# FFT convolution on one core: four weight differences half a round later, one plane burst half a round sooner, the first inverse jobs from half round 13

## The chip, the cores and the metric

The kernel runs on one core of a Trainium2 chip. The metric is the device time of one execution in microseconds. The core has five engines that run their own instruction streams: TensorE (PE, matrix products into PSUM; its weight loads are PEld), VectorE (DVE), ScalarE (ACT), GpSimd (POOL) and SyncE (SP), which issues nearly all DMAs here. An instruction that depends on another engine waits on a semaphore, and everything behind it on its own engine waits with it.

## The reference

The input `x` is 1 x 224 x 224 x 96 in bfloat16, the weights `w` are 7 x 7 x 96 x 96. Both are transformed over the image axes, multiplied per frequency with a sum over the input channels, and transformed back: a circular 7 x 7 convolution.

```python
wp = jnp.pad(w, ((0, H - K), (0, W - K), (0, 0), (0, 0)))
Xf = rfft2(x, axes=(1, 2))
Wf = rfft2(wp, axes=(0, 1))
Yf = jnp.einsum('bhwi,hwio->bhwo', Xf, Wf)
y = irfft2(Yf, s=(H, W), axes=(1, 2)).astype(jnp.bfloat16)
```

## The kernel before

The kernel does not transform the whole image. It splits the height into 8 blocks of 28 rows and works along the height with a short real transform of length 32 and two rows treated apart, which makes 17 "slots" s (slot 0 holds the two real frequencies, slots 1 to 15 are complex, slot 16 holds the two rows), and along the width it computes a direct 7-tap convolution in a two-phase form with few products. The width is split into 7 tiles t of 32 columns. For each tile there are four kinds of work:

- forward jobs (`f_jobs` for the first three tiles, `a_jobs` for the others): TensorE multiplies a loaded piece of x (`xn`) by the transform `Fm` into a PSUM bank, and `evac` copies the bank to `xf` on VectorE or ScalarE, whichever has the smaller running cost (the table `load`, to which VectorE's and ScalarE's other work is added as well);
- plane jobs (`jit`): three VectorE instructions per group of slots (`JGB`: 0-2, 3-5, 6-8, 9-11, 12-14, 15-16) that make sums and differences of `xf` in one of three buffers `J`;
- rounds (`b_round`): the products of one slot (TensorE, 33 matmuls of 96 columns for a complex slot), and their combination: ScalarE scales a part (`tt_`), VectorE makes `u` and `v` from PSUM, GpSimd adds them into `yf` (the y sum). After a group of slots `yf` is stored to the scratch `scr` in memory;
- inverse jobs (`c_jobs`): a transposed piece of the scratch (`tt`) is loaded, multiplied by the inverse transform `Gm` (two matmuls of 384 columns a job), evicted to `yo` and stored to the output. `yo` lies partly in the third J buffer, so the profile shows some as J. When a job is the last of its load, `pump` issues the next load.

The weights are transformed on the chip too. `prep_jobs` fill the first two of the three parts of each slot's weights `WF` (TensorE and an eviction), and `diff(i)` (line 400) makes the third part of slot i, the difference of the other two, in one VectorE instruction of 96 x 960. It adds 560 to VectorE's running cost.

The first two tiles run interleaved: in round r the first tile does slot r and the second tile slot r-4 (`LAG`). I call the two halves (r,0) and (r,1); rounds 4 to 16 have both. The filling work is put into half rounds by a small planner: `add(a, b, jobs)` spreads jobs over half rounds a to b (`pace`, line 828), and `fills` emits what is due. In the rounds that have both halves, (r,0) has the number 2r and (r,1) has 2r+1, and all that is due is emitted at `mid` (line 659): after VectorE's `u` and ahead of the products b1 and of VectorE's `v`. From the third tile on, one tile runs alone and slot s has the half rounds 2s (at `mid`) and 2s+1 (at `end`).

Per complex half round TensorE does: b0, with four matmuls on J, eight on xf (the last four use the difference) and seven on J (these use the third plane job); the fills; and b1, fourteen on J. VectorE does u, the fills that fall to it, v, and the plane jobs of a burst. Program order is kept on every engine (`_Ordered`).

A burst is one group's plane jobs: `bursts` (lines 851-859) gives the half round in which the first two instructions are emitted, behind `v`; the third follows in the next half round (`rest`, line 911). In a half round with two plane jobs the y sum on GpSimd is made to wait for them (line 677). The bursts around the change are: first tile, slots 9-11 in (7,1), 12-14 in (10,1), 15-16 in (13,1); second tile, slots 12-14 in (15,0), 15-16 in (16,0).

Difference i (5 to 15) is emitted in half round 2i-2, that is at the middle of (i-1,0) (line 866), and first used in (i,0). The loads of the first tile's scratch are issued in round 20 (`queue_c(0)`, line 904). While the third tile runs alone (t = 2), the 11 inverse jobs of the first tile are spread over half rounds 10 to 34 (lines 936-940, `CQ[2]` is (11, 0)).

Of the kernel before, what the change touches and what calls it, by code (L numbers as in the profile page):

```python
# [17 lines left out]
NS = L // 2  # L18
# [22 lines left out]
JGB = ((0, 3), (3, 6), (6, 9), (9, 12), (12, 15), (15, 17))  # L41
# [18 lines left out]
def slot(s, part):  # L60
    return S5[s][part] if s < len(S5) else 3 * s - 1 + part
# [3 lines left out]
def kernel(  # L65
# [10 lines left out]
    TL = NT - 1  # L76
# [67 lines left out]
    def dma(out_ap, in_ap):  # L144
        return DE.dma_start(out=out_ap, in_=in_ap)
# [43 lines left out]
    def load_x(t, jg):  # L189
        return load_rows(xbuf(t, jg), jg, t * 2 * TW, 2 * TW)  # L190
# [209 lines left out]
    def diff(s):  # L400
        def f():
            load["v"] += 60 + C * NTAP / 1.92
            w0, w1, w2 = (WF[0:C, slot(s, r)].rearrange("i t o -> i (t o)") for r in range(3))
            VE.tensor_tensor(out=w2, in0=w0, in1=w1, op=ALU.subtract)
        return f
# [69 lines left out]
    def new_xf(t, s0=0, s1=NS):  # L475
        xf = xf_bufs[t % 2]
        xf_tiles[t] = xf
        if t > 0:
            prev = xf_tiles[t - 1]
            for ph in range(2):  # L480
                o, i = (v[0:C, ph, :, s0:s1, p:p + HALO, :].rearrange("c r s w j -> c r s (w j)") for v, p in ((xf, 0), (prev, TW)))
                apart(("A", t), ("halo", s0), SE.copy(out=o, in_=i))
                load["a"] += 160 + 0.85 * 2 * (s1 - s0) * HALO * NJ
        return xf
# [34 lines left out]
    def then_load(f, t, jg):  # L519
        def g():  # L520
            f()
            if t < NT:
                load_x(t, jg)
        return g
# [11 lines left out]
    def f_jobs(t, part):  # L536
        s0, s1 = (SH0, SH2, SH3)[t][part:part + 2]
        n = 2 * (s1 - s0) * JG
        nr = -(-TW * n // 512)
        e = [-(-TW * i // nr) for i in range(nr + 1)]  # L540
        fv = Fm[:, :, s0:s1].rearrange("p r s j -> p r (s j)")

        def mk_(jg, a, b, ph):
            def f():
                pa = bank()
                for k in range(b - a):
                    i = 2 * (a + k) + ph
                    TE.matmul(pa[:, k * n:(k + 1) * n], lhsT=xbuf(t, jg)[:, i * C:i * C + 128], rhs=fv, start=True, stop=True)
                xo = xf_tiles[t][0:C, ph, :, s0:s1, HALO + a:HALO + b, jg * JG:(jg + 1) * JG]
                pi = pa[0:C, 0:(b - a) * n].rearrange("c (w r s j) -> c r s w j", r=2, s=s1 - s0, w=b - a)  # L550
                return apart(("A", t), (a, jg, ph, part), evac(xo, pi, (b - a) * n))
            return f
        return [[mk_(jg, a, b, ph) for a, b in zip(e[:-1], e[1:]) for ph in range(2)] for jg in range(2)]
# [247 lines left out]
    def queue_c(t):  # L801
        pend.extend((t, *k) for k in (LT if t < TL - 1 else LTL))
        pump()
# [32 lines left out]
    def fills(qs, k):  # L836
        def f():
            for q in qs:
                pace(q, k)
        return f  # L840
# [3 lines left out]
    def add(a, b, jobs):  # L844
        qs.append([a, b, jobs, len(jobs)])
# [5 lines left out]
    bursts = {}  # L851
    rest = []
    for g in range(len(JGB)):
        g0 = JGB[g][0]
        if g:
            bursts[(g0 - 2, 1 if g0 - 2 >= LAG else 0)] = (0, g)
        r1 = LAG + g0 - (3 if g == len(JGB) - 1 else 1)
        bursts[(r1, 0 if r1 < NS else 1)] = (1, g)
    bursts[(NS + LAG - 3, 1)] = (2, 0)
    nburst = len(bursts)  # L860
    for r in range(NS + LAG):
        if r == 0:
            for i in range(1, PGRP[0][1]):
                add(max(2 * i - 3, 0), 2 * i - 1, [diff(i)])
            for i in range(N5, REAL[1]):
                add(2 * i - 2, 2 * i, [diff(i)])
            add(0, 4, fj[1][0] + fj[1][1])
            add(8, 12, fj[2][0] + fj[2][1])
        if r == 2:
            new_xf(1, SH2[0], SH2[1])  # L870
        for p in range(3):
            if r == (1, 3, 6)[p]:
                if p:
                    new_xf(1, SH2[p], SH2[p + 1])
                else:
                    xf_tiles[1] = xf_bufs[1]
                fj = f_jobs(1, p)
                if p == 2:
                    for jg in range(2):
                        fj[jg][-1] = then_load(fj[jg][-1], 2, jg)  # L880
                add((4, 7, 12)[p], (7, 11, 15)[p], fj[0] + fj[1])
        for p in range(2):
            if r == SH3[p + 1] + 1 - p:
                new_xf(2, SH3[p], SH3[p + 1])
                fj = f_jobs(2, p)
                if p:
                    for jg in range(2):
                        fj[jg][-1] = then_load(fj[jg][-1], 3, jg)
                add(2 * r, 2 * r + (12, 5)[p], fj[0] + fj[1])
        if r == PGRP[-2][1] + 1:  # L890
            assert not any(q[2] for q in qs[:len(PGRP) - 1])
            wtmp_cm.__exit__(None, None, None)
            t_pool = ctx.enter_context(tc.tile_pool(name="tt", bufs=NTT, side="right"))
            t2_pool = ctx.enter_context(tc.tile_pool(name="tt2", bufs=1, side="right"))
            yo_pool = ctx.enter_context(tc.tile_pool(name="yo", bufs=2, side="right"))
            g_pool = ctx.enter_context(tc.tile_pool(name="gp", bufs=1, side="right"))
            GA = g_pool.tile([KA, 4 * B], BF16, name="GA")
            GB = g_pool.tile([128, 2, 4 * B], BF16, name="GB")
            GE.memset(GA[:], 0.0)
            GE.memset(GB[:], 0.0)  # L900
        if r == 3:
            g_fin()
        if r == NS + 3:
            queue_c(0)
        for t in range(2):
            s = r - LAG * t
            if not 0 <= s < NS:
                continue
            now = bursts.pop((r, t), ())
            now = jit(*now) if now else []  # L910
            now, rest = rest + now[:2], now[2:]
            both = LAG <= r < NS
            b_round(t, s, fills(qs, 2 * r + (t if both else 0)), fills(qs, 2 * r + (t if both else 1)), False, now)
            if r == 0:
                for d in load_x(1, 1):
                    tc.add_manual_dep(d.ins, held_x.ins.name, SYNC, reason="second half behind the first products")
# [8 lines left out]
    for t in range(2, NT):  # L925
        if t == TL:
            scr_tiles[t] = None
            scr_tiles[(t, 0)] = dr_pool.tile([TW, NJ, SA, 4 * C], BF16, name="scra")
            for i in range(2):
                scr_tiles[(t, 1 + i)] = dr_pool.tile([TW, NJ, (SB - SA, NS - SB)[i], 4 * C], BF16, name=f"scrb{i}")  # L930
        else:
            scr_tiles[t] = dr_pool.tile([TW, NJ, NS, 4 * C], BF16, name="scr")
        qs = []
        if t + 1 < NT:
            add(4 if t == 2 else 0, 26, a_jobs(t + 1))
        nold, nnew = CQ[t]
        k1 = 2 * NS if t < TL else 2 * NS - 8
        k0 = {2: 10, TL: 6}.get(t, 3)
        km = k0 + -(-(k1 - k0) * nold // (nold + nnew))
        add(k0, km, cj[:nold])  # L940
        cn = c_jobs(t - 1)
        cj = cn[nnew:]
        add(km, k1, cn[:nnew])
        plan = {}
        for g, (s0, s1) in enumerate(JGB):
            if g + 1 < len(JGB) or t + 1 < NT:
                plan[s0 if g + 1 < len(JGB) else s0 - 1] = g
        for s in range(NS):
            now = ()
            if s in plan:  # L950
                g = plan[s]
                now = jit(t, g + 1) if g + 1 < len(JGB) else jit(t + 1, 0)
            if s == (3 if t in (2, TL) else 2):
                queue_c(t - 1)
            if t in (3, 4):
                next(gp, None)
            if t == TL and s == SA + 2:
                sv = scr_tiles[(TL, 0)].rearrange("w j s (r e) -> (j s r) w e", r=2)
                for g in range(2):
                    for p0, p1 in ((0, 64), (64, KA)):  # L960
                        dma(tl_a[g][p0:p1], sv[g * KA + p0:g * KA + p1])
            b_round(t, s, fills(qs, 2 * s), fills(qs, 2 * s + 1), bool(now) or (t == TL and s >= NS - 3), now)
# [70 lines left out]
```

## Time and profile before

| what | us |
|---|---|
| median of 3 runs | 266.95 |
| lowest and highest | 266.09, 269.16 |
| profiled execution | 266.45 |
| its span | 264.7 |
| TensorE busy | 249.9 |
| VectorE busy | 219.5 |
| ScalarE busy | 196.2 |
| GpSimd busy | 98.6 |
| granted TensorE clock | 0.999 of full speed |

Times within the execution are counted from the start of the span. In a timeline, a line gives the start, the time from the first start to the last end, the engine, the line, the operation with output and inputs, how many instructions are merged, and in brackets the idle time of the engine before it and what ended it. All instructions show L99, the helper that keeps the order, so they are told apart by their tiles: WF<-WF is a difference, J<-xf and J<-J are plane jobs, yf<-v,u is a y sum, pb<-tt,Gm is an inverse job. In the profile round (8,0) has its u at 50.77, (11,0) at 63.44, (14,0) at 75.63, and (5,0) at 37.07.

### The profile page before, as it was taken

To read this page: it belongs to the slowest core of one execution; us is meant where nothing else is said; L and a number is where in the kernel's file an instruction comes from. 1 tells how busy PE (TensorE), PEld (TensorE's weight loads), DVE (VectorE), ACT (ScalarE), POOL (GpSimd) and SP (SyncE) were. 2 spreads that over 40 slices of the span, in tenths; PEclk is the share of its full clock that TensorE was granted. 3 is DMA by queue.
4 is the path that set the end of the run, shared out by engine and by line. 5 is a ranking of instruction groups with operands and counts; after the bars stand their busy time and mean duration, and the time that the engine had idled before them with its cause. 6 is when DMAs were issued, how large, how long until landed. Compare 5 with 4: busy or idle time off the path is not lost.

```text
span 264.7 us, 11951 instructions
## 1 busy us (share of the span) xinstructions
PE 249.9 (94%) x5041; PEld 232.0 (88%) x5041; DVE 219.5 (83%) x465; ACT 196.2 (74%) x467; POOL 98.6 (37%) x152
## 2 busy tenths in 40 slices
PE   8988999999998997999999999999999999999793
PEld 3978999999998996999999998999999999989472
DVE  6989898899899685778887888878989799989734
ACT  8979887787834966998988789897988853453433
POOL 7784134464655523323223232334123423424000
PEclk9999999999999999999999999999999999999999
DMA  7994105511113594997976596989689342858896
GB/s 184 275 190 112 47 6 157 157 47 47 50 46 122 145 233 86 276 302 205 304 211 210 140 279 193 249 242 308 204 167 272 103 138 83 224 171 203 227 247 207
DMA packets 46929, 46.77 MB, mean 177 GB/s; under 512 B 35340, under 2 KB 38104, under 8 KB 46876
## 3 DMA queue, kind: packets, MB, share of 16 engines
q1 hardware_dynamic: 46156, 44.54, 61.3%
q10 hardware_dynamic: 720, 1.47, 1.6%
q8 instruction: 39, 0.64, 1.0%
q14 instruction: 14, 0.11, 0.1%
HBM read 24.66 MB, written 21.33 MB: 174 GB/s over the span
## 4 chain that ended last, share of the span: by engine, by line
PE 70%; DVE 8%; DMA 7%; ACT 5%; issue 5%; POOL 2%; SPq 1%; DVEq 0%; POOLq 0%; ACTq 0%
PE pb L99 68%; DMA tt<-scr 5%; DVE J L99 3%; DVE v L99 2%; ACT xf L99 2%; PE ps L99 2%; ACT WF L99 2%; POOL ct L99 2%; DMA out_dram<-yo 1%; DVE WF L99 1%; SPq L99 1%; POOL yf L99 1%; DVE u L99 1%; DVE yf L99 0%; DVE wq L99 0%
## 5 line engine op out<-in xcount | busy, mean ns | idle before, releaser
L99 PE MATMUL pb<-WF,J 96*128 96x96 bf16 x2821 | 162.6, 206 | 2.5 <-DVE J L99 2.3
L99 PEld LDWEIGHTS <-J 96*128 96x128 bf16 x2821 | 137.4, 98 | 11.4 <-DVE J L99 3.6
L99 POOL TENSOR_TENSOR yf<-v,u 128x384 bf16<-128x384 f32 x79 | 81.7, 1046 | 140.8 <-issue 80.0
L99 ACT CAST xf<-pb 96x408 bf16<-96x408 f32 (+6 forms) x140 | 65.1, 491 | 3.5 <-PE pb L99 1.5
L99 PE MATMUL pb<-WF,xf 96*128 96x96 bf16 x952 | 60.1, 206 | 0.9 <-ACT WF L99 0.9
L99 DVE TENSOR_TENSOR J<-xf 96x456 bf16<-96x456 bf16 (+3 forms) x85 | 56.6, 705 | 0.0
L99 PEld LDWEIGHTS <-xf 96*128 96x128 bf16 x952 | 47.3, 98 | 1.4 <-ACT xf L99 0.8
L99 PE MATMUL pb<-Fm,xn 118*128 118x136 bf16 (+4 forms) x576 | 43.7, 203 | 0.9 <-ACT WF L99 0.9
L99 PE MATMUL pb<-tt,Gm 102*84 102x384 bf16 (+1 forms) x132 | 31.9, 326 | 2.5 <-DMA tt<-scr 1.8
L99 ACT CAST yo<-pb 84x384 bf16<-84x384 f32 (+1 forms) x59 | 25.2, 480 | 8.9 <-PE pb L99 5.6
L99 ACT CAST J<-pb 84x384 bf16<-84x384 f32 (+1 forms) x63 | 27.3, 491 | 4.9 <-PE pb L99 2.6
L99 PEld LDWEIGHTS <-xn 118*128 118x128 bf16 x576 | 28.6, 97 | 1.1 <-issue 0.9
L99 DVE TENSOR_TENSOR J<-J 96x912 bf16<-96x912 bf16 (+2 forms) x42 | 24.4, 580 | 0.0
L99 ACT CAST WF<-pb 96x480 bf16<-96x480 f32 x42 | 21.1, 561 | 0.3 <-PE pb L99 0.2
L99 PEld LDWEIGHTS <-wq 128*128 128x128 bf16 (+1 forms) x288 | 19.7, 149 | 0.7 <-ACT wq L99 0.7
L99 DVE TENSOR_TENSOR yf<-v,u 128x384 bf16<-128x384 f32 x26 | 15.1, 582 | 0.9
L99 PE MATMUL pb<-wq 128*128 128x120 bf16 x192 | 15.3, 224 | 0.0
L99 PEld LDWEIGHTS <-Gm 102*84 102x84 bf16 (+1 forms) x132 | 11.5, 117 | 4.1 <-issue 2.1
L99 DVE TENSOR_TENSOR WF<-WF 96x960 bf16<-96x960 bf16 x15 | 13.8, 918 | 1.4 <-ACT WF L99 1.3
L99 ACT COPY xf<-xf 96x816 bf16<-96x816 bf16 (+4 forms) x18 | 10.8, 652 | 0.0
L99 PEld LDWEIGHTS <-wu 128*112 128x112 bf16 (+1 forms) x36 | 4.6, 130 | 4.8 <-issue 2.5
L99 POOL TENSOR_SCALAR J<-J 102x1 f32<-102x1 f32 (+1 forms) x24 | 7.6, 316 | 1.8
(397 smaller groups left out, 252.6 us busy)
## 6 DMA issues: line engine op xcount, KB each, us to landing
scr<-yf SPq DMA_DIRECT2D x30, 288.0 KB
xn<-in_x_dram SPq DMA_DIRECT2D x12, 672.0 KB
tt<-scr SPq DMA_DIRECT2D x24, 336.0 KB
out_dram<-yo SPq DMA_DIRECT2D x12, 252.0 KB
out_dram<-J SPq DMA_DIRECT2D x12, 252.0 KB
tt<-scr SPq DMA_DIRECT2D x6, 288.0 KB
WF<-in_x_dram SPq DMA_DIRECT2D x2, 672.0 KB
out_dram<-tt SPq DMA_DIRECT2D x8, 168.0 KB
```

The costliest lines, as they stand in the source:

```text
L99: r = fn(*a, **k)
```

## The change

Three lines change. Differences 6, 9, 12 and 15 are emitted in half round 2i-1, at the middle of (i-1,1), instead of 2i-2. The second tile's burst for slots 12-14 is emitted in (14,1) instead of (15,0) (its third instruction in (15,0) instead of (15,1)); the other entries of `bursts` keep their values, since every r1 is below NS. The first tile's 11 inverse jobs are spread over half rounds 13 to 34 of the third tile instead of 10 to 34.

```diff
@@ -855,7 +855,7 @@
         if g:
             bursts[(g0 - 2, 1 if g0 - 2 >= LAG else 0)] = (0, g)
         r1 = LAG + g0 - (3 if g == len(JGB) - 1 else 1)
-        bursts[(r1, 0 if r1 < NS else 1)] = (1, g)
+        bursts[(r1 - 1, 1) if g == len(JGB) - 2 else (r1, 0)] = (1, g)
     bursts[(NS + LAG - 3, 1)] = (2, 0)
     nburst = len(bursts)
     for r in range(NS + LAG):
@@ -863,7 +863,7 @@
             for i in range(1, PGRP[0][1]):
                 add(max(2 * i - 3, 0), 2 * i - 1, [diff(i)])
             for i in range(N5, REAL[1]):
-                add(2 * i - 2, 2 * i, [diff(i)])
+                add(2 * i - (1 if i % 3 == 0 else 2), 2 * i, [diff(i)])
             add(0, 4, fj[1][0] + fj[1][1])
             add(8, 12, fj[2][0] + fj[2][1])
         if r == 2:
@@ -935,7 +935,7 @@
             add(4 if t == 2 else 0, 26, a_jobs(t + 1))
         nold, nnew = CQ[t]
         k1 = 2 * NS if t < TL else 2 * NS - 8
-        k0 = {2: 10, TL: 6}.get(t, 3)
+        k0 = {2: 13, TL: 6}.get(t, 3)
         km = k0 + -(-(k1 - k0) * nold // (nold + nnew))
         add(k0, km, cj[:nold])
         cn = c_jobs(t - 1)
```

## The prediction

> **What bounds the kernel now.** I read the page first, then TensorE's timeline for its idle times, then VectorE's and GpSimd's timelines around each of them. The profiled execution took 266.45 us with a span of 264.7, so 1.75 lies around the span; the median of the runs shown is 266.95, 0.5 above the profiled run.
>
> ```profile
> span 264.7 us, 11951 instructions
> PE 249.9 (94%) x5041; PEld 232.0 (88%) x5041; DVE 219.5 (83%) x465; ACT 196.2 (74%) x467; POOL 98.6 (37%) x152
> PEclk9999999999999999999999999999999999999999
> ```
>
> TensorE is busy 94% at full clock, so a gain must come out of its 14.8 us of idle time. Its timeline names all the idle places between 26 and 230 us (start, length, what ran, idle time before it and what ended it):
>
> ```profile
> 53.58 0.47 PE L99 MATMUL pb<-WF,J 96*128 96x96 bf16 x7 [0.31 <-DVE J L99]
> 66.26 0.47 PE L99 MATMUL pb<-WF,J 96*128 96x96 bf16 x7 [0.17 <-DVE J L99]
> 78.09 1.24 PE L99 MATMUL pb<-WF,J 96*128 96x96 bf16 x25 [0.37 <-DVE J L99]
> 82.98 1.24 PE L99 MATMUL pb<-WF,J 96*128 96x96 bf16 x25 [0.94 <-DVE J L99]
> 101.80 0.49 PE L99 MATMUL pb<-tt,Gm 102*84 102x384 bf16 x2 [1.83 <-DMA tt<-scr]
> ```
>
> Four waits are for plane jobs (J) and one for the first inverse job's data (tt). A listed idle time is 0.16 short of what is lost: matmuls start every 43 ns and their modelled length is 206 ns. So the losses are 0.47, 0.33, 0.53, 1.10 and 1.99, and 0.16 more at 77.4, before the second four matmuls of half round (15,0), which use difference 15. Together 4.58 us: all that this change can take away. The chain of waits shows how the first arises:
>
> ```profile
> 50.46 0.38 DVE J L99
> 50.84 0.27 DVE u L99
> 51.11 1.10 DVE WF L99
> 52.21 0.23 issue
> 52.44 0.54 DVE v L99
> 52.97 0.56 DVE J L99
> 53.53 0.05 issue
> 53.58 7.73 PE pb L99 x172
> ```
>
> Half round (8,0) puts difference 9 (WF) ahead of v and of the third plane job of slots 9 to 11, for which TensorE waits in (9,0). The timelines of VectorE and GpSimd show why WF is slow there:
>
> ```profile
> 50.98 1.02 POOL L99 TENSOR_TENSOR yf<-v,u 128x384 bf16<-128x384 f32 x1 [1.50 <-issue]
> 51.03 1.48 DVE L99 TENSOR_TENSOR WF<-WF 96x960 bf16<-96x960 bf16 x1
> 52.44 0.54 DVE L99 SCALAR_TENSOR_TENSOR v<-tt__1525,pb 128x384 f32<-128x384 f32 x1
> 52.90 0.62 DVE L99 TENSOR_TENSOR J<-J 96x912 bf16<-96x912 bf16 x1
> ```
>
> A difference alone takes 0.64 (the one at 37.34). This one took 1.48, as GpSimd's y sum (50.98 to 52.00) had started 0.05 before it; it ended 0.51 after the sum. The two engines exclude each other here: the one that started second waits. u and v, which read PSUM, are not held up. In the other order GpSimd waits: its sum of (8,0), in line at 53.05, ended at 54.40, 0.88 after the plane job.
>
> **Differences 6, 9, 12, 15 (half a round later).** Nothing is added or removed: four instructions move from the middle of (i-1,0) to the middle of (i-1,1), behind u and ahead of v of that half round. Their deadline does not move: the second four matmuls on xf in (i,0). So I replay VectorE with the rows' lengths, consecutive records overlapping by 0.08.
>
> Difference 9: v(8,0) 51.03 to 51.57; third plane job asked for at 51.49, held by the sum until 52.00, done 52.50. GpSimd's next sum, of (8,0), is in line since 51.57 and takes its turn after the plane job: done 52.50+0.88=53.38. u(8,1) 52.43 to 52.77 (its ScalarE input is there at 52.15). Difference 9 now comes at 52.69, under that sum: done 53.38+0.51=53.89. The sequence "held plane job, u, difference" exists in the trace at 58.33, 59.24 and 59.99, where the difference ended at 60.70, 1.39 after the plane job: 52.50+1.39=53.89, the same. TensorE wants it at 52.93 (the xf matmuls start at 52.76), so the loss is 1.00 instead of 0.47: +0.53.
>
> Difference 12, likewise: plane job held by the sum that ended at 64.68, done 65.18; sum of (11,0) done 66.06; difference done 66.57; wanted at 65.76. Loss 0.85 instead of 0.33: +0.52.
>
> Difference 15: short plane job (0.30) done about 77.05, after the sum that ended at 76.83; next sum done 77.9; difference done 78.4; wanted at 77.23. Loss 1.2 instead of 0.53+0.16: +0.5.
>
> Difference 6: no loss today. The balance between VectorE and ScalarE (evac) is followed through the code: with 560 not yet charged for the difference, one 320-element eviction of (5,0) goes to VectorE (0.47) in place of ScalarE; in (6,0) one 480-element eviction goes the other way. At the other three the margins are above 1,500, so nothing flips. Then u 37.07, two evictions, v ending 38.68, plane job to 39.2, the held sum to 40.06, difference to 40.57, wanted at 39.95: +0.62.
>
> In sum +2.2. Ends: without any hold by GpSimd the four would end at 40.06, 53.33, 66.01 and 77.86, which makes about 0 in sum; if GpSimd got in twice, 1.7 more (a rival below). I take 2.2, since each hold repeats one in the trace.
>
> One rule bears on these terms. The Trainium skill, "SBUF — State Buffer", section "Who interferes with whom", says that a VectorE instruction with two SBUF inputs and a GpSimd instruction that reads SBUF cannot run together, and that the second to issue stands still until the first is through. By its letter a held difference would end a whole 0.64 behind the sum and not 0.51, which would make four times 0.13, 0.5 us, more; the trace agrees with the exclusion (0.64 against 1.48) and not with that tail.
>
> **Planes of the second tile's slots 12 to 14 (half a round sooner).** Three instructions (1.10+0.38 and a third of 0.62, held 0.97) move from (15,0)/(15,1) to (14,1)/(15,0). The half round is free of planes, and its buffer was last read in (14,0). Their two-job part delays GpSimd's sum of (14,1) instead of that of (15,0). With difference 15 late, v(14,1) ends near 78.9, the two jobs near 80.2, its sum 81.3, the third job 81.8. TensorE wants the third at 82.08 plus the shift of 0.5 just found, so the wait goes: -1.10. If it did not, 0; more than 1.10 it cannot be.
>
> **Inverse jobs of the first tile from half round 13.** Eleven jobs move (22 matmuls, 22 evictions, 8 stores on the DMA queue and five calls for the next loads). The first one or two go from half rounds 10 and 12 to 13 and 14; the last ends at 32, not 31. Cover for the late load: from 99.81, where TensorE stopped, to half round 13 lie the rows from 102.13 to 104.88 less the job at 103.89 (0.33), so 2.42; it arrives at 102.23. The load is there by 101.66: 0.57 to spare, and both move together with what came before, as the load's issue (92.81) waits behind a store that waited for GpSimd's sum and input loads that waited for TensorE. What is late next: with 8 PSUM banks and four taken per round, b0 of round 6 wants the bank of u(4), free at 100.8, at 100.58: 0.2 back. I take -1.8. Ends: -1.99, and 0 if another load were late. On the DMA queue the first store and the first reload pass behind the input loads issued at 110.64, the second store behind one write of yf, and the second tile's loads come up to 2 half rounds later; they are not used before the next tile's half round 3, so I cost this at nothing. Density rises from 11 in 24 to 11 in 21 half rounds of 1.04 us: 22 evictions, whose starts are 0.37 apart, take 0.37 of ScalarE's time instead of 0.33, and it is 90% busy (22.47 of 25.00 us from 109), so this stays covered.
>
> From 102 to 246 TensorE is idle for 0.72 us in all (the table by stage), so the shift reaches the end unless a transfer there comes late.
>
> Sum: +2.2-1.1-1.8 = -0.7; 266.45-0.7 = 265.7.
>
> **The rivals.** *The differences cost nothing* (A): the sums leave them room, the terms are 0-1.1-1.8 = -2.9: 263.5. Against it, the pattern at 58.33 to 60.70. *All does what it could* (B): all five waits go, -4.58: 261.9. Against it, difference 9 cannot start before u(8,1), whose ScalarE input comes at 52.15. *The load stays late* (C): the wait of 1.8 moves to half round 13 or to the second tile's loads: 266.45+2.2-1.1 = 267.5, slower. It decides once the load lands later than 102.23 on the clock of before. Against it, 0.57 of room; for it, DMA engines busy all of their time from 94 to 100 (shares of 1.01, 1.33 and 1.20 by stage). *GpSimd gets in twice* (D): where a plane job is waiting and a sum ends, the next sum goes first; each of three differences ends 0.5 to 0.65 later, +1.7: 267.4, slower. It decides at 52.00. Against it, three places (46.02, 58.79, 71.47) where the waiting plane job went first.
>
> **How the numbers follow.** Forecast 0.52, A 0.19, B 0.07, C 0.13, D 0.09. One per cent is 2.7 us, about what a measurement of this kernel can tell from no change: below 263.8 or above 269.1. A and B give faster, with a little of the forecast's spread and less a little of A's, 0.25; slower by over 1% needs C and D together, 0.05; same 0.70. The range takes in A, C and D and leaves out B and the combination: 262.8 to 268.0. The likeliest case's own range is 264.9 to 266.6 (its terms: 1.7 to 2.7, -1.1, -1.99 to -1.6).
>
> **What would show it.** Right: at about 53, 65.8 and 77.3, TensorE waits for DVE WF instead of J, by 0.7 to 1.1 as listed; moved differences last over 1 us, under a sum; a new wait near 40; no wait near 83 and none at the first inverse job, which comes after 102. Wrong: moved differences of 0.65, or TensorE waiting for tt again. A gain of 2.9 or more would mean that my replay of the two engines' order failed; a loss, that the loads or the order of the lock did.

## The result, and the profile after

The changed kernel takes 268.49 us in the median (266.74 to 270.48, 22 executions); the kernel before, measured beside it, 266.02 (264.11 to 269.16, 22 executions). The ratio is 1.0081, 95% interval 1.0058 to 1.0104: 2.15 us slower, outside the forecast range. (A figure in us behind a ratio is the ratio times the time of before; the two medians as they stand can differ from it by up to 0.8.) The profiled execution took 267.38. Its page:

```profile
span 265.7 us, 11953 instructions
PE 251.7 (95%) x5041; PEld 233.0 (88%) x5041; DVE 219.6 (83%) x465; ACT 195.5 (74%) x467; POOL 98.3 (37%) x152
PEclk9999999999999999999999999999999999999979
```

The busy sums hardly moved but for TensorE's, which is 1.8 higher, most of it from matmuls at half clock near the end of this execution (below). The timeline of TensorE shows where it now waits between 26 and 230 us:

```profile
40.32 0.33 PE L99 MATMUL pb<-WF,xf 96*128 96x96 bf16 x4 [0.89 <-DVE WF L99]
54.31 0.33 PE L99 MATMUL pb<-WF,xf 96*128 96x96 bf16 x4 [0.81 <-DVE WF L99]
67.39 0.33 PE L99 MATMUL pb<-WF,xf 96*128 96x96 bf16 x4 [0.59 <-DVE WF L99]
79.74 0.33 PE L99 MATMUL pb<-WF,xf 96*128 96x96 bf16 x4 [1.03 <-DVE WF L99]
102.94 0.22 PE L99 MATMUL pb<-WF,J 96*128 96x96 bf16 x1 [0.77 <-issue]
```

All five old waits are gone. In place of three of them stand four waits for a difference, before the last four matmuls on xf, and a stop near 103 that no semaphore ended ("issue"). VectorE and GpSimd around the second of them, two views of the changed kernel:

```profile
51.89 0.99 DVE L99 TENSOR_TENSOR J<-J 96x912 bf16<-96x912 bf16 x1
52.81 0.34 DVE L99 SCALAR_TENSOR_TENSOR u<-pb,tt__1587 128x192 f32<-128x192 f32 x1
53.08 1.18 DVE L99 TENSOR_TENSOR WF<-WF 96x960 bf16<-96x960 bf16 x1
54.18 0.54 DVE L99 SCALAR_TENSOR_TENSOR v<-tt__1587,pb 128x384 f32<-128x384 f32 x1
```

```profile
51.38 2.36 POOL L99 TENSOR_TENSOR yf<-v,u 128x384 bf16<-128x384 f32 x2 [1.54 <-issue]
```

The second of GpSimd's two sums ends at 53.74, 51.38 plus 2.36. The difference came at 53.08, under it, and ended at 54.26, 0.52 behind it; TensorE went on at 54.31. Plane job, u and difference follow each other as the replay of the prediction had them.

Set matmul against matmul, the two traces give the account of one execution each. The same xf matmuls of round 5 of the third tile start 0.66 later; 0.68 of the other sign arose before anything had been changed (most of it in a wait for ScalarE near 25.9, of 0.86 in the trace before and 0.25 in the one after). The four differences added 1.05, 0.50, 0.42 and 0.50, the planes took off 1.10. Then 2.32 goes: 1.99 for the wait at the first inverse job, and 0.33 for that job itself, which now comes later. The stop near 103 gave back 0.94. By 200 us the two are level, and the 0.87 that is left at the end arises in the tail, behind 250 us, where TensorE ran at half clock for 3.4 us.

### The profile page after: what moved, and what is told of

Same layout as the page of the kernel before. It is cut to its first block, busy times and chain, and to the rows that moved or that the text cites. A ratio compares the mean times of both kernels' runs of the same rounds, so it can differ in the third digit from the quotient of the medians.

```text
span 265.7 us, 11953 instructions
## 1 busy us (share of the span) xinstructions
PE 251.7 (95%) x5041; PEld 233.0 (88%) x5041; DVE 219.6 (83%) x465; ACT 195.5 (74%) x467; POOL 98.3 (37%) x152
## 4 chain that ended last, share of the span: by engine, by line
PE 68%; DVE 11%; DMA 10%; issue 4%; ACT 3%; SPq 1%; POOL 0%; DVEq 0%; ACTq 0%
PE pb L99 67%; DVE J L99 4%; DMA WF<-in_x_dram 3%; DVE WF L99 2%; DVE v L99 2%; DMA tt<-scr 2%; DMA scra<-yf 2%; DMA out_dram<-yo 2%; DMA wq<-in_w_dram 2%; ACT xf L99 1%; SPq L99 1%; DVE u L99 1%; DVE yf L99 1%; ACT WF L99 1%; DMA scr<-yf 1%
## 5 line engine op out<-in xcount | busy, mean ns | idle before, releaser
L99 ACT CAST xf<-pb 96x408 bf16<-96x408 f32 (+5 forms) x141 | 65.5, 490 | 3.2 <-PE pb L99 1.3
L99 ACT CAST J<-pb 84x384 bf16<-84x384 f32 (+1 forms) x61 | 26.5, 488 | 4.3 <-POOL yf L99 2.3
L99 ACT CAST WF<-pb 96x480 bf16<-96x480 f32 x43 | 21.7, 566 | 0.0
L99 DVE TENSOR_TENSOR WF<-WF 96x960 bf16<-96x960 bf16 x15 | 12.5, 834 | 1.5 <-ACT WF L99 1.4
L99 PEld LDWEIGHTS <-wu 128*112 128x112 bf16 (+1 forms) x36 | 5.6, 158 | 6.1 <-issue 3.3
L99 DVE CAST tt<-pb 112x384 bf16<-112x384 f32 x8 | 4.1, 553 | 5.9 <-PE pb L99 5.7
## 6 DMA issues: line engine op xcount, KB each, us to landing
out_dram<-yo SPq DMA_DIRECT2D x12, 252.0 KB
out_dram<-J SPq DMA_DIRECT2D x12, 252.0 KB
```

The costliest lines, as they stand in the source:

```text
L99: r = fn(*a, **k)
```

## The experiments

Theory S: the time is the sum of TensorE's waits. Theory K: the changed kernel also loses clock. Theory T: the loss lies in the inverse jobs. Every ratio is against the kernel before on the same chip.

**The kernel before once more.** No edit.

> The kernel before once more, for its spread and its granted clocks over several executions. All theories: ratio 1.000 within 0.003. Theory S (the time is the sum of TensorE's waits in the trace) expects the granted clock to be about as low in it as in the changed kernel (mean 0.992 over 22 executions there). Theory K (the changed kernel loses clock on top of its waits) expects a mean granted clock of 0.996 or more here.

Measured: 1.0026 (0.9990 to 1.0061), 266.54. Twelve executions had granted clocks of 0.987 to 0.997, mean 0.992, the same as in the changed kernel: theory K falls. The clock goes with part of the spread within a kernel (264.44 us at 0.997, 268.02 at 0.987), not with the step between the two. The surprise is TensorE's timeline at the first inverse job:

```profile
99.67 0.49 PE L99 MATMUL pb<-tt,Gm 102*84 102x384 bf16 x2
101.82 0.33 PE L99 MATMUL pb<-WF,J 96*128 96x96 bf16 x4 [0.25 <-issue]
102.17 0.49 PE L99 MATMUL pb<-tt,Gm 102*84 102x384 bf16 x2
```

There is no wait for the load. The 1.83 us of the profile shown belonged to that execution. The tables by stage of the two executions tell why its time looked ordinary (columns: stretch, length, then busy time and number of instructions of PE, PEld, DVE, ACT and POOL, granted clock, DMA share, GB/s); first the profile shown, then this one:

```profile
250.60:254.00 3.40, 1.90 (x12) 1.55 (x13) 1.02 (x2) 0.85 (x2) 0.00 (x0) 1.00 1.17 237
```

```profile
250.60:254.00 3.40, 3.40 (x13) 2.31 (x12) 0.00 (x0) 0.00 (x0) 0.00 (x0) 0.50 1.04 212
```

Here the tail ran at half clock for 3.4 us, there not: one execution lost about 2 us at the load, the other 1.7 at its end (an estimate: half of the 3.4 us at half clock).

**The differences alone.**

```diff
-                add(2 * i - 2, 2 * i, [diff(i)])
+                add(2 * i - (1 if i % 3 == 0 else 2), 2 * i, [diff(i)])
```

> Only the four differences half a round later. Theory S: four waits for DVE WF of 1.05, 0.98, 0.76 and 1.19 in place of the waits for DVE J at 53, 66 and 78, the one at 83 and the one for the load kept: +2.5 us, ratio 1.009. Theory K: the same waits, and more executions with a granted clock under 0.995, so up to 2 us on top: 1.009 to 1.016. Theory T (the loss comes from the third tile's inverse jobs): the same waits as S, ratio up to 1.009, clock as before.

Measured: 1.0120 (1.0083 to 1.0157), 268.49: +3.2 us (2.2 to 4.2); the two medians differ by 2.4. TensorE waits for DVE WF by 0.55, 0.82, 0.59 and 1.03 as listed, and for DVE J by 0.94 at 85.5, as before at 83. Against the waits of before, these come to +2.1 us in this trace, so about 1 us of the middle value is in no wait that the trace shows. No wait for the load here either. The loss is this part.

**The planes alone.**

```diff
-        bursts[(r1, 0 if r1 < NS else 1)] = (1, g)
+        bursts[(r1 - 1, 1) if g == len(JGB) - 2 else (r1, 0)] = (1, g)
```

> Only the plane burst of the second tile's slots 12 to 14 half a round sooner. S and T: the wait of 0.94 at 83 goes and nothing takes its place: -1.1 us, ratio 0.996. K: the same, or up to -1.5 if the wait also cost clock.

Measured: 0.9968 (0.9934 to 1.0001), 265.34: -0.85 us, the interval reaching to zero. The trace has no wait at 83, and the waits at 53, 66 and 78 as before (the one at 66, where 0.31 is lost, is just below what the timeline lists).

**The inverse jobs alone.**

```diff
-        k0 = {2: 10, TL: 6}.get(t, 3)
+        k0 = {2: 13, TL: 6}.get(t, 3)
```

> Only the inverse jobs of the first tile from half round 13. S: the wait of 1.83 for the load goes; 1.99 gained, less up to 0.9 if TensorE then stops near 103 without a semaphore as in the changed kernel, and up to 0.6 given back by 180: -0.5 to -1.8 us, ratio 0.993 to 0.998. K: the same waits, clock 0.996 or more. T: slower, ratio 1.004 or more, with waits or a lower clock behind 100 us.

Measured: 0.9991 (0.9960 to 1.0021), 266.43: nothing that can be told from no change, neither S's gain nor T's loss. The trace has the stop:

```profile
101.94 0.22 PE L99 MATMUL pb<-WF,J 96*128 96x96 bf16 x1 [0.91 <-issue]
```

**Planes and inverse jobs**, the change without its first part.

> The change without its first part: planes sooner and inverse jobs from half round 13, differences as before. Theory S (the differences are the whole loss, the planes the whole gain, the inverse jobs nothing): the wait at 83 gone (-1.1 us), TensorE stopping without a semaphore near 101 for about 1 us as with the inverse jobs alone: ratio 0.995 to 0.998. If the parts act on each other (the planes sooner pay only with the late differences), ratio 1.000 or more.

Measured: 0.9968 (0.9934 to 1.0002), 265.14, the same as the planes alone. The parts add up within these intervals, and the inverse jobs add nothing that can be seen. The stop foreseen near 101 is nearly absent in this trace: 0.11 at 99.62.

**The late difference ahead of GpSimd's sum.** The differences as in the change, but the sum (and the store) of (i-1,0) is emitted in (i-1,1) behind the difference and waits for it.

```diff
+            if later:
+                later.pop(0)()
...
+                def late_sum():
+                    y = ysum(GE)
+                    tc.add_manual_dep(y.ins, last_diff[0].ins.name, SYNC, reason="sum after difference")
+                    put()
+                later.append(late_sum)
```

> The four differences half a round later as in the change, but the y sum of (i-1,0) is emitted behind the difference and waits for it, so GpSimd cannot be running when the difference comes. Theory G (a difference is late because GpSimd's sum holds it): differences of 0.64 in place of 1.2 to 1.4, waits for DVE WF of 0.1 to 0.6 in place of 0.8 to 1.2, time back by about 2 us: ratio 1.000 to 1.005. Rival O (its place behind u alone makes it late): waits of 0.8 to 1.1 stay, ratio 1.010 to 1.014.

Measured: 0.9981 (0.9948 to 1.0013), 265.32, against 1.0120 with the sum in its old place, and a little below the range of theory G. (Its executions had a mean granted clock of 0.996, those of before beside them 0.993; by estimate, 0.003 of 265 us, that could be 0.8 us.) All four moved differences take 0.64. VectorE around the second, and TensorE's waits for differences and for the load:

```profile
53.25 0.99 DVE L99 TENSOR_TENSOR J<-J 96x912 bf16<-96x912 bf16 x1
54.17 0.34 DVE L99 SCALAR_TENSOR_TENSOR u<-pb,tt__1585 128x192 f32<-128x192 f32 x1
54.44 0.64 DVE L99 TENSOR_TENSOR WF<-WF 96x960 bf16<-96x960 bf16 x1
```

```profile
41.70 0.33 PE L99 MATMUL pb<-WF,xf 96*128 96x96 bf16 x4 [0.33 <-DVE WF L99]
55.13 0.33 PE L99 MATMUL pb<-WF,xf 96*128 96x96 bf16 x4 [0.27 <-DVE WF L99]
79.70 0.33 PE L99 MATMUL pb<-WF,xf 96*128 96x96 bf16 x4 [0.63 <-DVE WF L99]
102.33 0.49 PE L99 MATMUL pb<-tt,Gm 102*84 102x384 bf16 x2 [0.60 <-DMA tt<-scr]
```

Same difference, same place behind u; only GpSimd's turn is another, and the waits fall to 0.33, 0.27 and 0.63 (the one near 67.8, where 0.31 is lost, is below the list). The wait of 0.94 for the planes, at 84.74, is there as before. That settles the cause: the hold by GpSimd makes a late difference dear; its place behind u costs the rest. The last line shows the load wait once more, 0.60 this time.

**The differences a round sooner**, to the middle of (i-2,0).

```diff
-                add(2 * i - 2, 2 * i, [diff(i)])
+                add(2 * i - (4 if i % 3 == 0 else 2), 2 * i, [diff(i)])
```

> Differences 6, 9, 12 and 15 a whole round sooner than before (the middle of (i-2,0)) instead of half a round later. Theory G: the third plane jobs are no longer held back, the waits for DVE J at 53, 66 and 78 go, none for DVE WF comes: -1.2 to -1.5 us, ratio 0.994 to 0.997. Rival: the half round they go to is then late in turn and the waits move one round ahead: ratio 0.998 to 1.002.

Measured: 0.9925 (0.9886 to 0.9965), 264.48: -2.0 us (-3.0 to -0.9), a little more than foreseen, with the foreseen value inside the interval. From 30 to 100 us TensorE's list holds only the wait of 0.93 at 82.09. The half rounds they go to had VectorE idle (0.40 and 0.31 in the timeline of before), so nothing is late in turn.

**Differences sooner, planes sooner** (both edits), measured twice.

> Differences a round sooner and the plane burst half a round sooner, inverse jobs as before. If the two add up: -2.3 to -2.6 us, ratio 0.990 to 0.993, and no wait of TensorE for VectorE from 30 to 98 us. If not, no better than the planes alone (0.997).

Measured: 0.9883 (0.9835 to 0.9931), 262.99, 6 executions: a little better than foreseen, with the foreseen 0.990 to 0.993 inside the interval.

> Differences a round sooner and planes half a round sooner once more, beside the run with the inverse jobs moved: ratio 0.988 within 0.004 if the first measurement holds; TensorE waiting for the first load at about 98 in at most one of such executions.

Measured: 0.9914 (0.9875 to 0.9954), 263.55, 12 executions. By the two measurements this is 0.9 and 1.2% faster than the kernel before, and so faster than the changed kernel as well. TensorE's whole list from 30 to 108 us in the profile of the first measurement:

```profile
98.85 0.33 PE L99 MATMUL pb<-WF,J 96*128 96x96 bf16 x4 [0.17 <-issue]
```

**The same with the inverse jobs from half round 13.**

> Differences a round sooner, planes half a round sooner, inverse jobs from half round 13: the changed kernel with its first part turned the other way. If the inverse jobs' part is worth nothing: ratio 0.986 to 0.991, with a stop of about 1 us near 100. If it is worth the 1.8 us that the prediction gave it: 0.981 to 0.984.

Measured: 0.9930 (0.9896 to 0.9964), 263.69, against 0.9914 without this edit. Again nothing from the inverse jobs: the 0.981 to 0.984 of a part worth 1.8 us is clearly missed, and the ratio is even a little above the 0.986 to 0.991 foreseen for a part worth nothing. The stop of 1 us foreseen near 100 is not there either.

**The stop near 102.** Theory F: TensorE runs out of instructions. First the inverse jobs from half round 22 with the loads in their place, then the same with the loads issued later, in round 6 of the third tile (the second tile's in round 7). Of each there is one execution.

```diff
-        k0 = {2: 10, TL: 6}.get(t, 3)
+        k0 = {2: 22, TL: 6}.get(t, 3)
```

```diff
-        if r == NS + 3:
-            queue_c(0)
...
-            if s == (3 if t in (2, TL) else 2):
+            if t == 2 and s == 6:
+                queue_c(0)
+            if s == {2: 7, TL: 3}.get(t, 2):
```

> Inverse jobs of the first tile from half round 22 of the third tile instead of 10, loads where they are. A control for the next run: with the loads' small packets filling the DMA engines from 94 to 103, theory F (TensorE runs out of instructions, as the fetch of its next piece stands behind those packets) expects TensorE to stop without a semaphore at about its matmul 2136 near 102, for 0.8 to 1.2 us. Rival (the stop belongs to the inverse jobs or to data): no stop there now that no job is near.

> The same, and the first tile's loads issued in round 6 of the third tile (the second tile's in round 7) instead of round 20. Theory F: no stop near matmul 2136, as the DMA engines are not full when its fetch comes; a stop may come later, at a fetch under the late loads. Rival (the stop belongs to this place in the instruction stream whatever the DMA engines do): the stop of 0.8 to 1.2 us stays at matmul 2136.

Measured: 269.03 and 271.48, slower than the 265.86 of before. Eleven jobs now crowd into twelve half rounds, and from 120 to 130 us TensorE is idle for 1.0 and 4.5 us, most of it waiting for ScalarE. In the control, the first of the two, the seven matmuls at 102.05 took 0.74 in place of the usual 0.46: a stop of 0.3 at matmul 2136, smaller than expected. With the loads moved it is gone. The two timelines of TensorE:

```profile
102.05 0.74 PE L99 MATMUL pb<-WF,J 96*128 96x96 bf16 x7
```

```profile
101.86 0.46 PE L99 MATMUL pb<-WF,J 96*128 96x96 bf16 x7
```

The times of single matmuls and packets tell more. Eight traces have the stop, of 0.11 to 1.07 us: before again, differences alone, inverse jobs alone, planes and inverse jobs, changed, jobs from 22, and both of the sooner pair. It always comes at matmul 2135 or 2136 of the program, in the middle of a product whose other operands are long there, and TensorE goes on 2.7 to 2.9 us after the 16th packet of the queue q8, of the kind "instruction", starts (for example 98.98 and 101.82, 101.47 and 104.28, 99.02 and 101.94, 100.01 and 102.94). In the six traces without it TensorE reaches that matmul no sooner than 2.8 us after the same packet's start. So in all 14 traces the matmul does not run before this packet has had its 2.7 us. The packet starts 6.9 to 8.5 us after the one before it in the 13 traces with the loads in place, and 5.3 us after it with the loads moved (91.28 and 96.60). So F is supported. That the loads' packets are what delays this one rests on a single execution, and the control's stop was smaller than foreseen; that half is not shown beyond doubt.

## Why the prediction was wrong

The step that failed is "Inverse jobs of the first tile from half round 13 ... I take -1.8". The edit alone measures -0.24 us (-1.1 to +0.6), and it adds nothing on top of the planes or of the sooner differences. The reading of the one profile was right, the wait of 1.83 was in it, but it is not what this kernel usually does: of eight profiled executions of kernels whose jobs start in half round 10, two wait for the load there (1.83 and 0.60) and six do not. In those two SyncE was held at the third of the tile's eight loads for 3.91 and 3.16 us, in the other six for 1.50 to 2.48; why it was is open. Where there is little to wait for, little can be gained. And TensorE, coming sooner to the same instruction, stops there for lack of the next ones: a stop that was in no term of the prediction. An estimate from the traces: over the eight executions the load costs 0.35 us in the mean and the stop 0.18; over the four whose jobs start in half round 13, the load costs nothing and the stop 0.53. That leaves nothing to gain, as measured, though so few executions fix neither mean well. Rival C had the size nearly right (267.5) and the mechanism wrong: the load was not late after the change, it had seldom been late before it. The range missed the median by 0.5 because it left out C together with a larger price for the differences.

By the prediction's own steps:

- The differences: +2.2 predicted; the trace after gives +2.5 (1.05+0.50+0.42+0.50), the trace of the edit alone +2.1, its time +3.2 (2.2 to 4.2). By the traces the size was right; by time it was too small, and what makes the rest is open. The mechanism is shown: the sum that holds the difference, the plane job that goes first, the wait for WF before the last four xf matmuls. Predicted losses were 0.62, 1.00, 0.85 and 1.2; lost, with 0.16 added to the listed idle times, were 1.05, 0.97, 0.75 and 1.19. The first was too low because in this execution TensorE came to that place 0.68 earlier and VectorE only 0.32 (its u at 36.75 instead of 37.07); in the edit alone 0.71 was lost there.
- The planes: -1.1 predicted, -1.10 in the trace, -0.85 by time.
- The sum of the three edits alone is 3.2-0.85-0.24 = +2.1, the change itself +2.15. No interaction is needed; with intervals of about 1 us on each, one of that size would not show.
- The rule of the Trainium skill ("SBUF — State Buffer", "Who interferes with whom") is borne out in its order and not in its tail. The four moved differences of the trace after ended 0.51 to 0.52 behind the sum that held them, not 0.64.
- The chances: the forecast had the wrong sign; "within 1%", which had 0.70, holds.

## What to carry to other kernels

A wait for a DMA in a single profile is one draw. Before its length is entered as a gain, ask whether the program makes it happen each time (an order of instructions does, a queue that is merely full does not), and look at a second execution if there is one. A small instruction on an engine that shares something with another engine has two durations (here 0.64 us alone and 1.0 to 1.5 under a sum), and where it is put decides which: move it to a place where the other engine is idle, here a round sooner, not to the last place that its deadline allows.

## What the runs showed of the hardware

TensorE's clock falls to half for single pieces of 3.41 us in a program that keeps it 95% busy: in the changed kernel at 252.0, after 1.24 us of idleness listed at 251.31, eleven matmuls on the tile `wu` (the kernel's loop `WARM`) were 0.32 apart instead of 0.16. The longest idle time alone does not decide it: the profile of before has 1.68 us of idleness at 252.10 and no such piece. Whether a given execution has one changes from run to run; the granted clock of the changed kernel as a whole varied between 0.976 and 1.000, with spans of 268.8 at the one end and 265.0 and 265.3 at the other. The Trainium skill, "TensorE: Matmul & The Clock Gate", section "Part 1: The HAM clock gate", gives the length as a free-running window of 3413 ns; the trace agrees with 3.41.

TensorE's instructions are themselves loaded by DMA in pieces: q8, of the kind "instruction" (39 packets, 0.64 MB), carries them, to judge by the 2.7 to 2.9 us between its 16th packet and TensorE's going on. A queue full of small packets (2,645 packets under 512 bytes from 97 to 104 us in the changed kernel) seems to delay a piece enough to stop the engine, here for 0.11 to 1.07 us in eight of 14 traces.
